# Sigmoid attention and two mixture layers on one core: PSUM banks, weight decoding and evictions rearranged

## The chip, the cores and the metric

The kernel runs on one core of a Trainium2 chip. The metric is the device time of one execution in microseconds (us). Engines are named as in the profile: PE is TensorE (matmuls; PEld its weight loads), DVE is VectorE, ACT is ScalarE, POOL is GpSimd, SP is SyncE, which here only issues transfers.

## The reference

Three stages follow each other. The inputs are fp32; batch 4, 12 heads, 448 positions, head size 64, so 1792 tokens of width 768.

```python
scores = q @ k.T / sqrt(64) - log(448);  x = sigmoid(scores) @ v      # per head
h = x @ w_in;  g = h - tanh(h);  x = g @ w_out                        # d_ff 2048, "layer one"
y = (sigmoid(x @ w_gate) * (x @ w_val)) @ w_out2                      # d_ff 1536, "layer two"
```

## The kernel before, in words

**Numbers.** Weights arrive as 64-bit floats and are read as pairs of 32-bit words. `decode()` (L114) turns a unit, a 128 x 768 part of a weight matrix, into fp32 words: piece a is one ScalarE pass (L121), b two VectorE passes (L124, L127), c two more (L133, L137) and the issue of a later unit's transfer. Matmuls run on fp32r pairs: each operand is kept as a high part (ScalarE copy) and a low part (operand minus high part), and each product is three matmuls (`mm3`, L300): high x high, high x low, low x high. `rounded()` (L145) makes the two parts of a weight, the low one by a GpSimd subtraction (L150).

**Attention** (24 head pairs) decodes the first seven units on the way. **Layer one** has 32 steps: 8 groups of two 128-column parts of `w_in`, for each of the four batches. Step i issues the hidden matmuls of step i+1 (`hidden_mm`, 36 matmuls, one PSUM tile of two banks), ScalarE's five passes for the activation (`hidden_act`, L322; squares, tanh, relu), and the output matmuls of step i: six groups of six matmuls (`project_group`, L370), each in one of four PSUM banks of the pool `psb`, each then added into an SBUF accumulator by VectorE (L381). Between the groups the list `extra` gives VectorE's pieces a to e of the activation and a decoding piece; f (L364), the low part of g, follows in the next step. Pieces run in program order on each engine.

**Layer two** has two passes over pairs of batches; each pass has six blocks. A block does seven products for the gate, then seven for the value (`TERMS`, nine matmuls each; the seven products replace eight, as in Strassen's scheme with Winograd's sums), and, spread over the gate half, twelve groups of six matmuls of the previous block's output projection ("fillers"). The operands s1 to s4 are sums and differences of halves of layer one's results (`operand`, L422); the weights t14, t32, b22 are differences made by VectorE (`ta`, `tb`). The four accumulators of a half lie in two tiles of two banks:

```python
pq = [psa.tile([128, 2, 512], F32, tag="pa", name=f"pq{j}") for j in range(2)]
pa, pb, pc, pe = (pq[j][:, i, :S] for j in range(2) for i in range(2))
bank = dict(a11=pa, s1=pe, s2=pb, a12=pa, s3=pc, s4=pb, a22=pc)
```

Sums shared by two products are copied from bank to bank by ScalarE (L575, L579 in `gate`; L593, L597 in `value`); VectorE closes a half with L583 and L585, or L599 to L611, and gg's low parts are two GpSimd subtractions of 128 x 896 (L606, L613).

In the first pass `background()` (L527), called after each product and each filler, hands out decoding pieces (`decode_pieces`) against a credit of time and at most one splitting piece (`split_pieces`) per call. A decoded pair of units is written to DRAM (`kept`, L471) and read again in the second pass (L476). Only pair 0 (two units) is decoded in the last steps of layer one. At the change of pass `turn()` makes the new operands, each in the place of one that is no longer needed.

Of the kernel before, what the change touches and what calls it, by code (L numbers as in the profile page):

```python
# [32 lines left out]
def kernel(  # L33
# [35 lines left out]
    stp = ctx.enter_context(tc.tile_pool(name="stp", bufs=2))  # L69
    dp = ctx.enter_context(tc.tile_pool(name="dp", bufs=1))  # L70
    psa = ctx.enter_context(tc.tile_pool(name="psa", bufs=2, space=bass.MemoryType.PSUM))
# [18 lines left out]
    MGAP = 16  # L90
    NPASS = NB // 2
# [13 lines left out]

    def fetch(u):
        if u >= len(units):
            return
        src, f = units[u]
        t = stp.tile([128, WC, 2], I32, tag="st", name=f"st{u}")  # L110
        nc.sync.dma_start(out=t.rearrange("p c w -> p (c w)"), in_=src[f])
        st_t[u] = t

    def decode(u, m):  # L114
# [28 lines left out]
        return [a, b, c]  # L143

    def rounded(w, mf, name, low=None):  # L145
# [4 lines left out]
        (low or nc.gpsimd).tensor_tensor(out=w1, in0=mf, in1=w0.bitcast(F32), op=ALU.subtract)  # L150

    def decode1(u):
# [7 lines left out]
        return decode(u, m) + [d]  # L160
# [161 lines left out]
    def hidden_act(i):  # L322
# [12 lines left out]
        nc.scalar.activation(out=uu, in_=h, func=AF.Square)  # L335
        nc.scalar.activation(out=y, in_=h, func=AF.Tanh)
        nc.scalar.activation(out=mk, in_=uu, func=AF.Relu, bias=gb[:, 2:3], scale=-1.0)
        nc.scalar.activation(out=s1, in_=mk, func=AF.Square, bias=gb[:, 0:1], scale=-1.0)
        nc.scalar.activation(out=s2, in_=mk, func=AF.Square, bias=gb[:, 1:2], scale=-1.0)
# [28 lines left out]
        return [a, b, c, d, e, f]  # L368

    def project_group(name, at, gt, outs, d, first, dst=None):  # L370

        po = psb.tile([128, 512], F32, tag="pb", name=name)
        for j, (_, w) in enumerate(outs):
            mm3(
                po[:, :S], lambda a: w[:, a, d], lambda a: gt[:, a, j],
                j == 0, j == len(outs) - 1,
            )
        if first:
# [8 lines left out]

    def groups1(i):

        g, t = divmod(i, NB)  # L390
        outs = [w_t[4 * g + 2], w_t[4 * g + 3]]
        gt = g_t.pop(i)
        if g == 0:
            acc[t] = acc_tile(t, f"acc{i}")
        for d in range(KD):
            def run(d=d):
                project_group(f"po{i}_{d}", acc[t], gt, outs, d, g == 0)
                if t == NB - 1 and d == KD - 1:
                    w_free.extend(n for n, _ in outs)
            yield run  # L400

    def project(i, extra):
        for group in groups1(i):
            group()
            if extra:
                extra.pop(0)()
        for f in extra:
            f()

# [11 lines left out]

    def operand(ps, term, low):  # L422
        a, b = acc[2 * ps], acc[2 * ps + 1]
        src = dict(
            a11=a[:, :KH], a12=a[:, KH:], a22=b[:, KH:], s1=b[:, :KH], s2=b[:, :KH],
# [3 lines left out]
        if term == "s1":  # L429
            nc.vector.tensor_tensor(out=b[:, :KH], in0=b[:, :KH], in1=b[:, KH:], op=ALU.add)  # L430
        elif term == "s2":
            nc.vector.tensor_tensor(out=b[:, :KH], in0=b[:, :KH], in1=a[:, :KH], op=ALU.subtract)
        elif term == "s3":
            nc.vector.tensor_tensor(out=a[:, :KH], in0=b[:, KH:], in1=b[:, :KH], op=ALU.subtract)
        elif term == "s4":
            nc.vector.tensor_tensor(out=b[:, :KH], in0=a[:, KH:], in1=b[:, :KH], op=ALU.subtract)
# [3 lines left out]
        low.tensor_tensor(out=t[:, 1], in0=src, in1=t[:, 0].bitcast(F32), op=ALU.subtract)  # L440

    m_t = {}
    kept = {}
    wk = {}
    done = {"slot": 0}
    decodes = []
    splits = []

    def pair_m(n):
        pool, tag = ((dp, "m"), (mp[0], "m2"))[n % 2]  # L450
        m_t[n] = pool.tile([128, 2 * WC], I32, tag=tag, name=f"mm{n}")
        return m_t[n]

    def decode_pieces(n):
        box = {}

        def start(h):
            if h == 0:
                pair_m(n)
            box[h] = decode(U2 + 2 * n + h, m_t[n][:, h * WC:(h + 1) * WC])  # L460

        def piece(h, s):
            def run():
                if s == 0:
                    start(h)
                box[h][s]()
                if h == 1 and s == 2:
                    done[n] = done["slot"]
                    if NPASS > 1:
                        kept[n] = keep_p.tile([128, 2 * WC], I32, tag=f"kept{n}", name=f"kept{n}")  # L470
                        nc.sync.dma_start(out=kept[n], in_=m_t[n])  # L471
            return run

        def again():
            pair_m(n)
            nc.sync.dma_start(out=m_t[n], in_=kept[n - 3 * NBLK])  # L476
            done[n] = done["slot"] + 3

        if n >= 3 * NBLK:
            return [(n, again, 0.0)]  # L480

        return [(n, piece(h, s), (0.2, 1.1, 1.9)[s]) for h in range(2) for s in range(3)]

    def split_pieces(n):
# [5 lines left out]
        def keep(key, lo, hi):  # L490
            def run():
# [9 lines left out]
                rounded(t, quarters(lo, hi), f"w{n}_{key}")  # L501
# [22 lines left out]
    credit = [0.0]  # L524
    last = [-9]

    def background(length):  # L527

        done["slot"] += 1
        now = done["slot"]  # L530
        credit[0] = min(credit[0] + length, 2.5)
        if splits:
            n, f, cost, room = splits[0]
            if n in done and done[n] + (cost > 0) < now and (not room or w_free):
                splits.pop(0)
                f()
                credit[0] -= cost
        while decodes and credit[0] > 0:
            n, f, cost = decodes[0]
            if any(s[0] <= n - 2 for s in splits):  # L540
                break
            decodes.pop(0)
            f()
            credit[0] -= cost
# [7 lines left out]
    def block(k, fillers):  # L552
# [4 lines left out]
        pa, pb, pc, pe = (pq[j][:, i, :S] for j in range(2) for i in range(2))  # L557
        bank = dict(a11=pa, s1=pe, s2=pb, a12=pa, s3=pc, s4=pb, a22=pc)

        def product(n, term):  # L560
            key, half = PRODUCT[term]
            s, w = wk[n, key]
# [10 lines left out]
        def gate(term):  # L573
# [6 lines left out]
            elif term == "a12":  # L580
                nc.scalar.activation(out=sg[0][:, 0], in_=pa, func=AF.Sigmoid)
            elif term == "s3":
                nc.vector.tensor_tensor(out=sg[1][:, 1], in0=pc, in1=p5[0], op=ALU.add)  # L583
            elif term == "s4":
                nc.vector.tensor_tensor(out=sg[0][:, 1], in0=pb, in1=p5[0], op=ALU.add)  # L585
                nc.scalar.activation(out=sg[1][:, 1], in_=sg[1][:, 1], func=AF.Sigmoid)
            elif term == "a22":
                nc.scalar.activation(out=sg[0][:, 1], in_=sg[0][:, 1], func=AF.Sigmoid)
                nc.scalar.activation(out=sg[1][:, 0], in_=pc, func=AF.Sigmoid)

        def value(term):
# [8 lines left out]
            elif term == "s3":  # L600
                nc.vector.tensor_tensor(out=pe, in0=pc, in1=p5[1], op=ALU.add)
            elif term == "s4":
                nc.vector.tensor_tensor(out=pb, in0=pb, in1=p5[1], op=ALU.add)
                nc.vector.tensor_tensor(out=sg[0][:, 1], in0=pb, in1=sg[0][:, 1], op=ALU.mult)
                nc.scalar.activation(out=gt[0][:, 0], in_=sg[0], func=AF.Copy)
                nc.gpsimd.tensor_tensor(  # L606
                    out=gt[0][:, 1], in0=sg[0], in1=gt[0][:, 0].bitcast(F32), op=ALU.subtract
# [251 lines left out]
```

## Time and profile before

| | us |
|---|---|
| median of 3 runs | 1260.87 (1260.05 to 1269.46) |
| the profiled execution's own time | 1250.63 |
| its span, first to last instruction | 1248.9 |
| PE busy | 1122.2 (90%) |
| DVE busy | 873.2 (70%) |
| ACT busy | 543.1 (43%) |
| POOL busy | 426.5 (34%) |

Times in rows are us from the span's start; durations of single instructions in groups are ns. A line such as `PE L302 MATMUL pq<-a,w_t ... [1.92 <-DVE sg L609]` says that TensorE stood idle for 1.92 us until VectorE's line 609 released it. PEclk is the granted share of TensorE's full clock (2.4 GHz; 0.5 is 1.2 GHz). A matmul's own duration overlaps with the next one's, so the pace is read from start to start.

### The profile page before, as it was taken

To read this page: it belongs to the slowest core of one execution; us is meant where nothing else is said; L and a number is where in the kernel's file an instruction comes from. 1 tells how busy PE (TensorE), PEld (TensorE's weight loads), DVE (VectorE), ACT (ScalarE), POOL (GpSimd) and SP (SyncE) were. 2 spreads that over 40 slices of the span, in tenths; PEclk is the share of its full clock that TensorE was granted. 3 is DMA by queue.
4 is the path that set the end of the run, shared out by engine and by line. 5 is a ranking of instruction groups with operands and counts; after the bars stand their busy time and mean duration, and the time that the engine had idled before them with its cause. 6 is when DMAs were issued, how large, how long until landed. Compare 5 with 4: busy or idle time off the path is not lost.

```text
span 1248.9 us, 15482 instructions
## 1 busy us (share of the span) xinstructions
PE 1122.2 (90%) x6085; PEld 995.5 (80%) x6085; DVE 873.2 (70%) x1150; ACT 543.1 (43%) x693; POOL 426.5 (34%) x288
## 2 busy tenths in 40 slices
PE   9999999999999999999566977877596899999998
PEld 5777799999999999988565866767485788988897
DVE  4778468888888888877886789678756444444343
ACT  6788535544445544444433333333325233323320
POOL 5555000111111111111663353435337555345431
PEclk9999999999999999999877989998998999999999
DMA  7666001111112111112034345442411322111202
GB/s 196 206 181 180 28 1 51 52 51 51 51 55 73 51 51 51 51 59 69 26 86 141 127 151 171 133 152 83 144 51 51 99 69 73 51 51 51 76 1 89
DMA packets 35017, 105.61 MB, mean 85 GB/s; under 512 B 5504, under 2 KB 20864, under 8 KB 34944
## 3 DMA queue, kind: packets, MB, share of 16 engines
q1 hardware_dynamic: 31712, 102.22, 25.4%
q0 software_dynamic: 3072, 2.17, 0.8%
q8 instruction: 48, 0.79, 0.2%
q14 instruction: 25, 0.20, 0.1%
q10 hardware_dynamic: 160, 0.23, 0.1%
HBM read 84.93 MB, written 19.66 MB: 84 GB/s over the span
## 4 chain that ended last, share of the span: by engine, by line
PE 69%; DVE 13%; issue 6%; ACT 4%; DMA 4%; POOL 4%; SPq 0%; ACTq 0%; POOLq 0%; DVEq 0%
PE pq L302 26%; PE po L302 17%; PE ph L302 17%; PE pv L286 4%; PE sa L251 3%; DVE mm L133 2%; POOL w_t L150 2%; DMA kept<-mm 2%; DVE mm L137 2%; DVE mm L124 1%; ACT mm L121 1%; PE sl L263 1%; DVE mm L512 1%; POOL w L150 1%; DMA st<-in_w_gate_dram 1%
## 5 line engine op out<-in xcount | busy, mean ns | idle before, releaser
L302 PE MATMUL po<-g,w 128*128 128x448 f32 x1152 | 238.4, 364 | 3.5 <-ACT g L361 2.3
L302 PE MATMUL ph<-x,w 128*128 128x448 f32 x1152 | 235.8, 362 | 0.2 <-ACT at L255 0.2
L302 PEld LDWEIGHTS po<-g,w 128*128 128x128 f32 x1152 | 217.4, 189 | 19.3 <-ACT g L361 2.7
L302 PEld LDWEIGHTS ph<-x,w 128*128 128x128 f32 x1152 | 215.8, 187 | 15.4 <-ACT at L255 0.6
L302 PE MATMUL pq<-gg,w 128*128 128x448 f32 x864 | 188.6, 368 | 4.3 <-DVE acco L381 2.6
L150 POOL TENSOR_TENSOR w<-m,w 128x768 fp32r<-128x768 f32 x32 | 59.3, 1853 | 381.1 <-ACT w L149 368.3
L302 PEld LDWEIGHTS pq<-gg,w 128*128 128x128 f32 x864 | 164.9, 191 | 18.0 <-DVE acco L381 4.2
L302 PE MATMUL pq<-s,w_t 128*128 128x448 f32 x648 | 147.9, 376 | 20.0 <-DVE y L360 8.9
L302 PEld LDWEIGHTS pq<-s,w_t 128*128 128x128 f32 x648 | 126.0, 196 | 32.8 <-ACT s L439 9.2
L381 DVE TENSOR_TENSOR acc<-po,acc 128x448 f32<-128x448 f32 x168 | 101.8, 618 | 52.8 <-PE po L302 52.8
L150 POOL TENSOR_TENSOR w_t<-mm,w_t 128x768 fp32r<-128x768 f32 x48 | 94.2, 1967 | 128.6 <-ACT w_t L149 128.6
L302 PE MATMUL pq<-a,w_b 128*128 128x448 f32 x432 | 106.8, 396 | 31.9 <-ACT pq L597 19.7
L302 PEld LDWEIGHTS pq<-a,w_b 128*128 128x128 f32 x432 | 89.1, 209 | 44.6 <-ACT pq L597 24.3
L381 DVE TENSOR_TENSOR acco<-pq,acco 128x448 f32<-128x448 f32 x120 | 72.7, 621 | 73.9 <-PE pq L302 73.9
L302 PE MATMUL pq<-a,w_t 128*128 128x448 f32 x216 | 59.4, 429 | 53.5 <-DVE sg L609 45.7
L302 PEld LDWEIGHTS pq<-a,w_t 128*128 128x128 f32 x216 | 46.7, 224 | 63.8 <-DVE sg L609 50.2
L150 POOL TENSOR_TENSOR w_b<-mm,w_b 128x768 fp32r<-128x768 f32 (+1 forms) x48 | 76.1, 1596 | 60.9 <-ACT w_b L149 58.6
L149 ACT ACTIVATE w_t<-mm 128x768 fp32r<-128x768 f32 x48 | 40.1, 841 | 103.2 <-DVE mm L512 61.8
L150 POOL TENSOR_TENSOR w<-mm,w 128x768 fp32r<-128x768 f32 x24 | 46.1, 1924 | 98.5 <-ACT w L149 78.8
L335 ACT ACTIVATE u<-ph 128x896 f32<-128x896 f32 x32 | 29.4, 918 | 115.9 <-PE ph L302 115.8
L255 ACT ACTIVATE at<-sa,bias_s 128x896 f32<-128x896 f32 x72 | 67.3, 1008 | 8.0 <-PE sa L251 8.0
L124 DVE TENSOR_SCALAR mm<-mm 128x768 f32<-128x768 f32 x36 | 32.9, 914 | 46.7 <-ACT mm L121 46.6
(90 smaller groups left out, 1634.0 us busy)
## 6 DMA issues: line engine op xcount, KB each, us to landing
st<-in_w_out_dram SPq DMA_DIRECT2D x28, 768.0 KB, 4.6
kept<-mm SPq DMA_DIRECT2D x18, 768.0 KB, 7.0
mm<-kept SPq DMA_DIRECT2D x18, 768.0 KB, 4.2
st<-in_w_in_dram SPq DMA_DIRECT2D x16, 768.0 KB, 4.4
st<-in_w_gate_dram SPq DMA_DIRECT2D x12, 768.0 KB, 4.4
st<-in_w_val_dram SPq DMA_DIRECT2D x12, 768.0 KB, 5.2
kt<-in_k_dram SPq DMA_DIRECT2D x48, 112.0 KB, 3.7
out_dram<-acco SPq DMA_DIRECT2D x24, 224.0 KB, 2.2
```

Of the source, the lines that this page charges most:

```text
L121: nc.scalar.activation(out=mf, in_=hi.bitcast(F32), func=AF.Abs)
L124: nc.vector.tensor_scalar(out=mf, in0=mf, scalar1=W_LOW, scalar2=W_HIGH, op0=ALU.max, op1=ALU.min)
L133: nc.vector.scalar_tensor_tensor(out=m, in0=hi, scalar=-0x40000000, in1=m, op0=ALU.bitwise_and, op1=ALU.bitwise_or,)
L137: nc.vector.scalar_tensor_tensor(out=m, in0=lo, scalar=29, in1=m, op0=ALU.logical_shift_right, op1=ALU.bitwise_or,)
L149: nc.scalar.activation(out=w0, in_=mf, func=AF.Copy)
L150: (low or nc.gpsimd).tensor_tensor(out=w1, in0=mf, in1=w0.bitcast(F32), op=ALU.subtract)
L251: nc.tensor.matmul(pa[:, j, :S], kk[r, ki, c], qq[r, qi], start=(i == 0), stop=(i == 2),)
L255: nc.scalar.activation(out=at[:, :, c], in_=pa[:, :, :S], func=AF.Sigmoid, bias=bias_s, scale=qk_scale,)
L286: nc.tensor.matmul(po[j * D:(j + 1) * D, h, :SH], vt[:, j, c], at[:, j, c, h * SH:(h + 1) * SH], start=False, stop=(c == NCH - 2),)
L302: nc.tensor.matmul(o, w(i), xv(j), start=first and n == 0, stop=last and n == 2, skip_group_check=seeded,)
L335: nc.scalar.activation(out=uu, in_=h, func=AF.Square)
L381: nc.vector.tensor_tensor(out=at[:, d], in0=po[:, :S], in1=at[:, d], op=ALU.add)
```

## The change

- **Banks.** `pa`, `pb`, `pc`, `pe` and the four banks of output groups become eight one-bank tiles of a new pool `pm`, opened after layer one. `gate` and `value` treat s3 and s4 in the order in which the products come; s3's two VectorE operations stand together.
- **Decoding.** All 36 units of layer two are listed in `early`, four pieces each (c is cut into c and c2). In layer one, steps 1 to 26 take a unit each, except those before step 24 whose number is a multiple of four; the rest is handed out by `background()`, one piece per call, then a pause of 4.0. Every decoded unit goes to DRAM and both passes read pairs by `load_m`. One staging buffer serves layer one's units and one layer two's (before: two for all).
- **Sums.** In layer one's steps 4 to 28, groups 1, 3 and 5 are seeded: ScalarE copies the accumulator into the PSUM bank ahead of the matmuls (`seed`) and copies the sum back (`post`), in place of VectorE's addition. ScalarE's passes of the activation are spread over the step.
- **GpSimd.** Subtractions of weights, gg and operands are cut in two or three; f moves from VectorE to GpSimd, b22's low part, some operands' and the last block's gg from GpSimd to VectorE.
- **Change of layer and pass.** s1 to s4 are sums of unchanged halves (`sums`) and are made earlier; fillers start after s2; `require()` makes a missing weight on the spot.

The core of the diff:

```diff
 def decode(u, m):
...
+        def c2():
             nc.vector.scalar_tensor_tensor(
                 out=m, in0=lo, scalar=29, in1=m,
...
-            fetch(u + 2)
+            fetch(follower(u))
...
 def rounded(w, mf, name, low=None):
...
-        (low or nc.gpsimd).tensor_tensor(out=w1, in0=mf, in1=w0.bitcast(F32), op=ALU.subtract)
+        for r in (slice(None),) if low else (slice(0, HC), slice(HC, None)):
...
 def hidden_act(i):
...
         def f():
-            nc.vector.tensor_tensor(
-                out=gt[:, 1], in0=y, in1=gt[:, 0].bitcast(F32), op=ALU.subtract
-            )
+            for j in range(2):
+                nc.gpsimd.tensor_tensor(
+                    out=gt[:, 1, j], in0=y[:, j], in1=gt[:, 0, j].bitcast(F32), op=ALU.subtract
+                )
...
+    def seed(name, at, d):
+        po = pb_tile(name)
+        nc.scalar.activation(out=po[:, :S], in_=at[:, d], func=AF.Copy)
+        return po
...
+    def step(i, act, dve, extra, po):
...
+        def pre(d):
+            if g and i < LASTSEED:
+                po[d] = seed(f"po{i}_{d}", at, d)
...
+        def post(d):
+            if i >= LASTSEED:
+                return
+            nc.scalar.activation(out=at[:, d], in_=po[d][:, :S], func=AF.Copy)
...
+        sq()
+        th()
+        group(0)
+        a()
+        pre(3)
+        cut()
+        group(1)
+        b()
+        run(ex[0] or [])
+        group(2)
+        q1()
+        post(1)
+        c()
+        run(ex[1] or [])
+        pre(5)
+        q2()
+        group(3)
+        d_()
+        run(ex[2] or [])
+        post(3)
+        group(4)
+        e()
+        run(ex[3] or [])
+        group(5)
+        post(5)
...
 def background(length, heavy=True):
...
+        if early and now > free_at[0]:
+            early.pop(0)()
+            if len(early) % 4 == 0:
+                free_at[0] = now + 4.0
...
 def block(k, fillers):
...
-        pa, pb, pc, pe = (pq[j][:, i, :S] for j in range(2) for i in range(2))
+        pa, pb, pc, pe = (
+            pm[0].tile([128, 512], F32, tag=f"p{c}", name=f"p{c}{k}")[:, :S] for c in "abce"
+        )
...
+        share = dict(s2=2, a12=4, s3=7, s4=10, a22=12)
...
+        def some(kind):
+            if early and len(early) % 4 == kind and (i < TAIL or kind) and (i % 4 or i > TAIL - 4):
+                early.pop(0)()
+
         for i in range(N1 - 1):
             hidden_mm(i + 1)
+            po = {}
+            if NB <= i < LASTSEED:
+                po[1] = seed(f"po{i}_1", acc[i % NB], 1)
             if todo:
                 todo.pop(0)()
             if rest:
                 rest.pop()()
             if todo:
                 todo.pop(0)()
-            extra = hidden_act(i + 1)
+            some(0)
+            some(3)
+            act, dve = hidden_act(i + 1)
...
+            if todo:
+                ex[0].append(todo.pop(0))
...
+                ex[2].append(todo.pop(0))
+            ex[1].append(lambda: some(2))
+            ex[2].append(lambda: some(1))
```

## Rows read from the trace of the kernel before

**Rows 1.** Windows: length, busy PE, PEld, DVE, ACT, POOL (counts), PEclk, DMA share, GB/s

```profile
146.00:560.00 414.00, 412.64 (x2080) 385.83 (x2081) 341.36 (x444) 199.67 (x222) 46.45 (x25) 1.00 0.14 48
560.00:601.00 41.00, 37.48 (x186) 34.20 (x185) 33.42 (x39) 22.26 (x24) 11.00 (x5) 1.00 0.19 58
601.00:680.00 79.00, 47.87 (x174) 41.07 (x173) 64.43 (x61) 26.29 (x36) 39.05 (x17) 0.76 0.31 100
680.00:855.00 175.00, 135.93 (x595) 119.01 (x595) 135.01 (x161) 60.78 (x90) 76.64 (x40) 0.90 0.42 135
...
1016.00:1229.00 213.00, 200.04 (x979) 183.92 (x978) 93.28 (x126) 66.64 (x103) 95.92 (x54) 0.99 0.13 45
```

**Rows 2.** TensorE's waits in layer two: us in total, times, longest

```profile
PE pq L302 <- DVE sg L609: 45.7, 12, 9.8
PE pq L302 <- ACT pq L597: 19.7, 12, 5.4
PE pq L302 <- ACT pq L579: 11.7, 2, 9.2
```

**Rows 3.** Timeline of the last block: start, us, engine, line [idle <-releaser]

```profile
1219.48 2.08 PE L302 MATMUL pq<-a,w_b 128*128 128x448 f32 x9 [0.68 <-ACT pq L597]
...
1227.08 2.57 PE L302 MATMUL pq<-a,w_t 128*128 128x448 f32 x9 [1.92 <-DVE sg L609]
...
1231.44 2.12 POOL L613 TENSOR_TENSOR gg<-sg,gg 128x896 fp32r<-128x896 f32 x1 [1.72 <-ACT gg L612]
```

**Rows 4.** Timeline of ScalarE: L575, once a block, of blocks 1, 5, 7, 11

```profile
679.96 0.53 ACT L575 ACTIVATE pq<-pq 128x448 f32<-128x448 f32 x1 [0.28 <-PE pq L302]
...
912.84 0.53 ACT L575 ACTIVATE pq<-pq 128x448 f32<-128x448 f32 x1
...
1015.66 0.53 ACT L575 ACTIVATE pq<-pq 128x448 f32<-128x448 f32 x1 [0.19 <-PE pq L302]
...
1188.24 0.53 ACT L575 ACTIVATE pq<-pq 128x448 f32<-128x448 f32 x1 [0.19 <-PE pq L302]
```

**Rows 5.** Decoding passes by line, layer two (mm) and before (m)

```profile
L133 DVE SCALAR_TENSOR_TENSOR mm<-st,mm 128x768 int32<-128x768 int32 x36 | 47.0, 1306 | 0.6
...
L127 DVE TENSOR_SCALAR mm<-mm 128x768 int32<-128x768 int32 x36 | 35.7, 992 | 1.2
...
L133 DVE SCALAR_TENSOR_TENSOR m<-st,m 128x768 int32<-128x768 int32 x32 | 30.4, 951 | 0.0
L121 ACT ACTIVATE m<-st 128x768 f32<-128x768 f32 x32 | 29.4, 917 | 52.6 <-POOL w L150 51.0 <-DMA st<-in_w_in_dram 1.6
...
L127 DVE TENSOR_SCALAR m<-m 128x768 int32<-128x768 int32 x32 | 17.9, 560 | 1.1
```

**Rows 6.** Timeline: a decoding pass beside GpSimd's subtractions

```profile
652.01 4.30 POOL L150 TENSOR_TENSOR w<-mm,w 128x768 fp32r<-128x768 f32 x2 [2.86 <-issue]
...
654.65 2.08 DVE L127 TENSOR_SCALAR mm<-mm 128x768 int32<-128x768 int32 x1
```

**Rows 7.** Timeline of one step of layer one

```profile
301.64 7.36 PE L302 MATMUL po<-g,w 128*128 128x448 f32 x36
...
305.48 1.03 ACT L339 ACTIVATE s<-mk,gb 128x896 f32<-128x896 f32 x1
...
312.47 1.09 DVE L364 TENSOR_TENSOR g<-y,g 128x896 fp32r<-128x896 f32 x1
...
316.04 7.36 PE L302 MATMUL po<-g,w 128*128 128x448 f32 x36
```

**Rows 8.** Timeline: first weight loads of two successive steps, end of layer one

```profile
563.29 0.19 PEld L302 LDWEIGHTS po<-g,w 128*128 128x128 f32 x1 [2.66 <-ACT g L361]
...
578.53 0.19 PEld L302 LDWEIGHTS po<-g,w 128*128 128x128 f32 x1
```

**Rows 9.** DMA issues: KB each, median us to landing

```profile
kept<-mm SPq DMA_DIRECT2D x18, 768.0 KB, 7.0
...
st<-in_w_gate_dram SPq DMA_DIRECT2D x12, 768.0 KB, 4.4
```

More of the change, by code (lines that the diff above doesn't have):

```diff
@@ L158, in d, with keeping, piece, run @@
             w_t[u] = n, w
-        return decode(u, m) + [d]
+        a, b, c, c2 = decode(u, m)
+        return [a, b, lambda: (c(), c2()), d]
+    kept = {}
+    early = []
+    def keeping(j):
+        box = []
+        def piece(s):
+            def run():
+                if s == 0:
+                    if late[0]:
+                        if not mq:
+                            mq.append(stp.tile([128, 2 * WC], I32, tag="st0", name="mq"))
+                        m = mq[0][:, j % 2 * WC:][:, :WC]
+                    else:
+                        m = wp.tile([128, WC], I32, tag="wh0", name=f"mk{j}")
+                    box.append(m)
+                    box.extend(decode(NU1 + j, m))
+                box[1 + s]()
+                if s == 3:
+                    n, h = divmod(j, 2)
+                    if h == 0:
+                        kept[n] = keep_p.tile([128, 2 * WC], I32, tag=f"kept{n}", name=f"kept{n}")
+                    nc.sync.dma_start(out=kept[n][:, h * WC:(h + 1) * WC], in_=box[0])
+                    whole.add(j)
+            return run
+        return [piece(s) for s in range(4)]
+    late = [False]
+    mq = []
+    whole = set()
     att_ctx = ExitStack()
@@ L424, in operand @@
         src = dict(
-            a11=a[:, :KH], a12=a[:, KH:], a22=b[:, KH:], s1=b[:, :KH], s2=b[:, :KH],
+            a11=a[:, :KH], a12=a[:, KH:], a22=b[:, KH:], s1=b[:, :KH], s2=a[:, :KH],
             s3=a[:, :KH], s4=b[:, :KH],
         )[term]
[L429 to L436, printed above, removed]
+        for other in (("s4", term) if term == "s3" else (term,)):
+            if other in ("s1", "s2", "s3", "s4") and (ps, other) not in summed:
+                sums(other, ps)
         t = x_tile(PLACE[ps][term], f"{term}_{ps}")
@@ L439, in operand, with load_m @@
         nc.scalar.activation(out=t[:, 0], in_=src, func=AF.Copy)
-        low.tensor_tensor(out=t[:, 1], in0=src, in1=t[:, 0].bitcast(F32), op=ALU.subtract)
+        for c in range(KH):
+            low.tensor_tensor(
+                out=t[:, 1, c], in0=src[:, c], in1=t[:, 0, c].bitcast(F32), op=ALU.subtract
+            )
     m_t = {}
-    kept = {}
     wk = {}
     done = {"slot": 0}
-    decodes = []
+    FETCH = 6.5
+    loads = []
     splits = []
-    def pair_m(n):
-        pool, tag = ((dp, "m"), (mp[0], "m2"))[n % 2]
-        m_t[n] = pool.tile([128, 2 * WC], I32, tag=tag, name=f"mm{n}")
[L452 to L482, printed above, removed]
+    order = [0, 1]
+    for blk in range(NK):
+        order += [n for n in (3 * blk + 3, 3 * blk + 2, 3 * blk + 4) if n < 3 * NK]
+    place = {n: at for at, n in enumerate(order)}
+    def load_m(n):
+        pool, tag = ((dp, "m"), (mp[0], "m2"))[place[n] % 2]
+        m_t[n] = pool.tile([128, 2 * WC], I32, tag=tag, name=f"mm{n}")
+        k = n % (3 * NBLK)
+        assert 2 * k + 1 in whole
+        nc.sync.dma_start(out=m_t[n], in_=kept[k])
+        done[n] = done["slot"] + FETCH
     def split_pieces(n):
@@ L633, in block @@
                 turn(ps + 1, term)
-            background(1.8 - {"a12": 0.6, "s3": 0.6, "s4": 1.8, "a22": 0.6}.get(term, 0.0))
+            background(1.8, term not in ("s4", "a22"))
             value(term)
@@ L721 @@
         assert not todo
[L722 removed]
+        for f in dve[3:]:
             f()
```

277 lines of the change are left out of this document (182 added, 95 removed).

## The prediction

> **What bounds the kernel now.** I read the stages first, then TensorE's waits, then the waits' places. A step of layer one does 72 matmuls; in steady state it takes 14.40 us, 0.200 us a matmul, and TensorE is busy without a gap and at the full clock (2.4 GHz, granted 1.00) [rows 1, 7]. Nothing is to be gained there. Layer two is another matter: 12 blocks of 198 matmuls plus the 36 left from layer one are 2,412 x 0.200 = 482 us, and it takes 1248.9 - 601 = 648 us. So 166 us lie in it, at VectorE's expense: its share of the time is 82% (64.43 of 79) and 77% (135.01 of 175) in the first pass, 44% (93.28 of 213) in the second [rows 1]. The start times of one copy per block (L575) give the profile of the loss: the first pass takes (912.84 - 679.96) / 4 = 58.2 us a block, the two blocks around the change of pass (1015.66 - 912.84) / 2 = 51.4, the second pass (1188.24 - 1015.66) / 4 = 43.1 [rows 4]. 198 x 0.200 = 39.6 would be the pace of TensorE alone. The entry is worst: 601 to 680 for 162 matmuls (32.4 us) and one product more (1.8).
>
> TensorE's waits name two lines above all: 45.7 us for L609 and 19.7 + 11.7 for the copies L597 and L579 [rows 2]. What these two wait for is not what the products need: the product a22 adds into pc, L609 reads pe; a12 adds into pa, the copies read pb and write pc. But pa, pb share one tile and pc, pe the other. In the last block, with VectorE idle enough, it costs 0.68 and 1.92 us still [rows 3].
>
> **The change, part by part.** *Banks.* With a tile for each accumulator, a22 waits only for L601, two VectorE operations and one product earlier; a12 only for the copy of pa, done one product (1.8 us) before. In the second pass 0.68 + 1.92 go from each value half, and up to 0.3 comes back: 43.1 becomes 40.2 a block, 39.6 plus 0.6 for the odd late copy. Order s3/s4 within gate() and value() now follows the order of the products, which puts no new wait in. What is late next is the true wait, a22 on L601, hidden as long as VectorE isn't over 1.2 us (1.8 - 0.62) late.
>
> *Decode.* A weight half (unit) costs VectorE four passes: 2 x 0.56 + 2 x 0.95 = 3.0 us in layer one, 2 x 0.99 + 2 x 1.31 = 4.6 in layer two [rows 5]. They are the same operations; the longer ones ran beside a GpSimd subtraction (L127: 2.08 us instead of 0.56, while L150 runs on GpSimd) [rows 6]. So far all but two of 36 units' passes fall in layer two, 6 a block, 27.6 us of VectorE in 58.2. The change decodes one unit in each step from 1 to 26 whose number isn't a multiple of four, and from 24 on in each: 21. 15 are left, one per about 10 us of background() time (four calls, then 4.0): some 3.9 a block, over in block 4, ahead of use (pair 10 is first needed by block 3). VectorE's sum in a first-pass block: 135.01 / 175 x 58.2 = 44.9 now; less 27.6, plus 3.9 units at 3.8 (midway, since GpSimd's pieces are half as long) = 14.8, plus 1 for the subtractions of b22 that move to it: 33, of 43.6 that I take for these blocks (75%, the same share as now at 58.2, where false waits added to it; 40.2 and 50 are the ends). Blocks 1 to 3: 43.6; block 4: 41.6.
>
> *Entry.* Here s1 and s2 are summed late; one wait for L579, the copy that follows the product s2, takes 9.2 us [rows 2]. The sums now come ahead of the last step, the four halves of weights are split two steps earlier, no unit is decoded in the first 16 us. I take 5 us of loss (0 to 15): 32.4 + 1.8 + 5 = 39 for the 79. *Change of pass.* The low parts of the operands for s1 to a22 (1,344 columns each) are cut in three, and s1's, s2's and s4's go to VectorE, which has decoding no more. 102.8 for two blocks becomes 87 (80.4 to 97).
>
> Layer two: 39 + 3 x 43.6 + 41.6 + 87 + 4 x 40.2 + 57.3 (the last 60.7 less 2.9 for its value half and 0.5 for VectorE's faster last low part) = 516.5 of 648: **-131**.
>
> *Layer one pays.* Per step, in effective pace: VectorE loses three of six evictions (0.54 each from start to start) and the low part of g (1.0), and gets a unit (3.0) in three of four steps. Now it is busy 341.36 / 414 = 82%, 11.9 us a step on the mean [rows 1], 12.4 in the steps that decode a unit for layer one (25 of the 29); then 12.4 - 1.6 - 1.0 + 3.0 = 12.8, below 14.4. ScalarE: 199.67 / 414 x 14.4 = 6.9 now, plus three seeds and three copies (0.53 each, the size of L575 [rows 4]) and 0.9 for the unit's first pass [rows 5]: 11.0. It too fits. What counts is the order. In the step of [rows 7], counted from the first group's start (301.64), the last square ends at 4.87, g's low part is done at 11.92 and needed at 14.40: 2.5 us to spare. In the changed queue the seeds of groups 3 and 5, group 1's copy back and a weight half's copy stand ahead of the last square (some 0.45 each and 0.75 from start to start): it ends at 7.0. Behind it come, on VectorE, one operation of 1.0, a unit's pass of 0.95, an eviction of 0.55 and the predicated copy of 1.1: 10.6; ScalarE's copy, 1.0: 11.6; two GpSimd pieces of 1.05 (a 128x896 subtraction takes 2.12 [rows 3]): 13.7. The second piece is needed at 15.0, after the group's first three matmuls. 1.3 us are to spare; what exceeds them TensorE waits, in every step anew.
>
> Two things can eat them. First, GpSimd's pieces and VectorE's decoding collide right there. [rows 6] show VectorE held until the subtraction ends. The Trainium skill, "SBUF — State Buffer", section "Who interferes with whom", says that a VectorE operation with two SBUF inputs and a GpSimd operation that reads SBUF exclude each other for the whole instruction, whoever starts first. By that rule moving g's low part speaks against this change: up to 2.1 us a step more for VectorE, 12.8 + 2.1 = 14.9, or 0.5 x 21 = 11 us in all. Second, the next unit's first pass stands on ScalarE ahead of the squares, and needs a transfer issued when the unit before is done (single buffers): 4.4 us, and the write-back of the decoded half, 7.0 for twice its size [rows 9]. The unit is done at about 9; with 4.4 and 0.9 the squares can start at 14.3, in time; with 7.0 and 0.9 at 16.9, 2.5 us late, in the 15 steps that follow a step with a unit. Queued behind it on ScalarE are the squares, the seeds and the copies; TensorE waits for these at the next group. Ends: 0, and 15 x 2.5 + 11 = about 48 with nothing to spare. I take **+8**: 1.3 us are to spare, and a step of four is free to catch up. A gain is excluded: TensorE has no gap there now. Edits without a price: attention (same two staging buffers until unit 6), the pools' new names.
>
> Own time of the profiled execution: 1250.6 - 131 + 8 = 1127.6. The median of the three runs shown is 1260.9, 10 above; forecast: **1138 us**.
>
> **Rivals.** *Layer one becomes the slower stage*: the transfer loop above decides in every step with a unit, +40 in place of +8: 1170. For it: a tail step that decodes for layer two already stretched to 578.53 - 563.29 = 15.24, the weight load waiting 2.66 for ScalarE's g [rows 8]. Against: there the pieces stood between every two operations. Chance 0.17. *VectorE stays the bound in the first pass*: 15 units and GpSimd's locks keep blocks 1 to 3 at 50, entry 45, block 4 at 46, the pass change at 97: +40, 1178. For it: 75% busy is much for an engine that is waited for in order. Chance 0.11. *The banks don't do what they say*: the wait passes on to L601 and to the copies, whose own lateness is the true cause; second-pass blocks stay at 43.1, first-pass ones lose 3 more each: 6 x 2.9 + 4 x 3 = 29, 1167. Against: in [rows 3] VectorE and ScalarE were free. Chance 0.10. *Slower than before*: layer one falls from the full clock. Now it runs at 1.00; where TensorE waits, 601 to 680, the granted clock is 0.76, a mean of stretches at 2.4 and at 1.2 GHz [rows 1]. A step at 0.76 takes 14.4 / 0.76 = 18.9; with 1 us of waiting +5.5 over 27 steps: +149 instead of +8, 1279. It decides from 131 / 27 = 4.9 us a step on. Against: the tail, with the wait of [rows 8], kept 1.00 (560 to 601) [rows 1]. Chance 0.04.
>
> **How the numbers follow.** The forecast holds 0.58: 1138, alone between 1115 and 1160 (first-pass blocks at 40.2 or 46, entry 0 to 15, layer one 0 to 15). The range takes in the three rivals' 1167 to 1178 and some of their sum: 1108 to 1190. About 1% of the time (12 us) is what a measurement of this kernel can tell from no change. All cases but the last are over 5% faster; the last, and a mixture of the first two rivals at their ends, give the rest: faster 0.94, same 0.02, slower 0.04.
>
> **What would show it.** Right: no wait on the line that succeeds L609, no a12 wait on the copy into pc; second-pass blocks at 40 to 40.5; first-pass ones at 42 to 46 with VectorE near 75%; TensorE's gap at the entry below 10 us; layer-one steps of 14.4 to 15 with VectorE about 88% and ScalarE 77% busy, GpSimd's waits beside c2. Wrong: layer-one steps above 15.5, or a granted clock below 1.00 there; first-pass blocks at 50; a22 waiting over 1 us for VectorE in the second pass.

## The result, and the profile after

The changed kernel takes 1127.72 us (median of 4 runs, 1127.19 to 1131.71), the kernel before 1260.46 (four runs; the 1260.87 above is of three): a ratio of 0.894, 95% interval 0.889 to 0.899. The forecast was 1138. The profiled execution has a span of 1125.4 us at a mean granted clock of 0.998 (before: 1248.9 at 0.959).

By stage, with the windows of the changed kernel (columns as in [rows 1]): layer one's middle, blocks 1 to 4, and the second pass.

```profile
142.00:530.00 388.00, 378.16 (x1872) 339.49 (x1871) 318.40 (x369) 252.95 (x358) 133.19 (x94) 1.00 0.31 100
661.00:824.00 163.00, 158.50 (x783) 146.20 (x784) 127.92 (x166) 69.39 (x104) 102.17 (x82) 1.00 0.46 154
910.00:1068.00 158.00, 158.00 (x792) 148.09 (x791) 77.18 (x112) 57.76 (x89) 85.12 (x80) 1.00 0.17 61
```

The counts of matmuls tell the pace: 388 / 1872 = 0.207 us in layer one, which was 0.199 before (414 / 2080 of [rows 1]); 158 / 792 = 0.199 in the second pass, where TensorE has no gap left. In the first pass some matmuls are missing from the trace (783 for four blocks of 198), so its pace is read from the marks below: 40.7 for a block's 198, 0.206 each.

The same marks as in [rows 4], from the timeline: the first product of layer two on TensorE, then L722 (L575 before) of blocks 1, 5, 7 and 11; the last line is the first product of layer two in the kernel before.

```profile
619.50 1.96 PE L365 MATMUL pa<-a,w_b 128*128 128x448 f32 x9
...
661.48 0.52 ACT L722 ACTIVATE pb<-pa 128x448 f32<-128x448 f32 x1
...
824.43 0.52 ACT L722 ACTIVATE pb<-pa 128x448 f32<-128x448 f32 x1
...
909.91 0.52 ACT L722 ACTIVATE pb<-pa 128x448 f32<-128x448 f32 x1
...
1068.31 0.52 ACT L722 ACTIVATE pb<-pa 128x448 f32<-128x448 f32 x1
```

```profile
601.18 1.97 PE L302 MATMUL pq<-a,w_b 128*128 128x448 f32 x9
```

| stretch, us | before | forecast | after |
|---|---|---|---|
| start to first product of layer two | 601.2 | 609 | 619.5 |
| entry and block 0, to block 1's L722 | 79 | 39 | 42.0 |
| blocks 1 to 4, mean of one | 58.2 | 43.1 | 40.7 |
| blocks 5 and 6 together | 102.8 | 87 | 85.5 |
| second pass, a block | 43.1 | 40.2 | 39.6 |
| last block's L722 to the end | 60.7 | 57.3 | 57.1 |

Layer two takes 506 us (forecast 516.5, before 648); layer one 18.3 more than before (forecast 8).

TensorE's waits from 618 on (us in total, times, longest). [rows 2] had 45.7, 19.7 and 11.7 at its head:

```profile
PE pc L365 <- DVE pe L761: 5.1, 3, 2.2
PE pb L365 <- ACT pb L722: 2.7, 4, 1.2
PE pq L365 <- POOL gg L742: 2.4, 2, 1.8
```

In layer one (145 to 600), ScalarE's wait for a transfer and the longest of the weight loads:

```profile
ACT mk L145 <- DMA kept<-mk: 40.8, 15, 3.9
...
PEld po L365 <- DVE acc L472: 10.9, 13, 1.1
PEld po L365 <- POOL g L437: 8.5, 20, 0.7
PEld po L365 <- ACT po L454: 3.8, 15, 1.1
```

Fifteen times ScalarE waited for the write-back of a decoded half: there are 15 steps with a unit that follow a step with a unit. One such step in the timeline: the write-back is issued at 318.05; ScalarE's pass for the next unit (L145, L121 before) starts at 323.69, and only then the first square (L399).

```profile
308.98 0.91 ACT L399 ACTIVATE u<-ph 128x896 f32<-128x896 f32 x1
...
318.05 0.43 SPq L215 DMA_DIRECT2D kept<-mk  x1
...
320.38 3.75 POOL L437 TENSOR_TENSOR g<-y,g 128x448 fp32r<-128x448 f32 x2 [5.49 <-issue]
...
321.32 1.79 DVE L163 SCALAR_TENSOR_TENSOR m<-st,m 128x768 int32<-128x768 int32 x1
...
323.69 0.89 ACT L145 ACTIVATE mk<-st 128x768 f32<-128x768 f32 x1 [2.57 <-DMA kept<-mk]
324.49 0.90 ACT L399 ACTIVATE u<-ph 128x896 f32<-128x896 f32 x1
...
338.89 0.92 ACT L399 ACTIVATE u<-ph 128x896 f32<-128x896 f32 x1 [2.27 <-PE ph L365]
```

The step from 308.98 to 324.49 takes 15.51, the next one, without a unit ahead of it, 14.40. The two GpSimd pieces of g take 3.75 together and VectorE's last decoding pass beside them 1.79 instead of 0.95.

A late unit's four passes on VectorE, by line (L148, L151, L157, L163 were L124, L127, L133, L137), 630 to 830:

```profile
L157 DVE SCALAR_TENSOR_TENSOR mq<-st,mq 128x768 int32<-128x768 int32 x15 | 21.1, 1410 | 0.1
...
L163 DVE SCALAR_TENSOR_TENSOR mq<-st,mq 128x768 int32<-128x768 int32 x15 | 17.4, 1163 | 0.1
L151 DVE TENSOR_SCALAR mq<-mq 128x768 int32<-128x768 int32 x15 | 16.2, 1079 | 0.5
L148 DVE TENSOR_SCALAR mq<-mq 128x768 f32<-128x768 f32 x15 | 12.2, 817 | 4.0 <-ACT mq L145 4.0
```

Together 4.47 us, beside 4.6 in [rows 5] and the 3.8 of the forecast. What the length of the pieces does to it is tested below.

### The profile page after: what moved, and what is told of

It reads as the page before. It is cut to its first block, busy times and chain, and to the rows that moved or that the text cites. A ratio compares the mean times of both kernels' runs of the same rounds, so it can differ in the third digit from the quotient of the medians.

```text
span 1125.4 us, 15990 instructions
## 1 busy us (share of the span) xinstructions
PE 1091.5 (97%) x6085; PEld 967.6 (86%) x6085; DVE 806.8 (72%) x1083; ACT 608.8 (54%) x855; POOL 522.7 (46%) x475
## 4 chain that ended last, share of the span: by engine, by line
PE 60%; DVE 14%; ACT 9%; DMA 9%; issue 5%; POOL 3%; SPq 1%; ACTq 0%; DVEq 0%; POOLq 0%
PE pq L365 14%; PE ph L365 10%; DMA kept<-mk 8%; PE pb L365 6%; PE po L365 6%; PE pa L365 6%; PE pc L365 5%; PE pv L349 5%; PE sa L314 4%; PE pe L365 3%; DVE ph L422 2%; DVE ph L427 2%; ACT mk L405 1%; ACT y L402 1%; PE sl L326 1%
## 5 line engine op out<-in xcount | busy, mean ns | idle before, releaser
L365 PE MATMUL po<-g,w 128*128 128x448 f32 x1152 | 247.7, 367 | 10.3 <-DVE acc L472 6.0
L365 PEld LDWEIGHTS po<-g,w 128*128 128x128 f32 x1152 | 211.7, 188 | 40.5 <-POOL g L437 11.6
L365 PEld LDWEIGHTS ph<-x,w 128*128 128x128 f32 x1152 | 215.8, 187 | 15.3 <-ACT at L318 0.6
L437 POOL TENSOR_TENSOR g<-y,g 128x448 fp32r<-128x448 f32 x64 | 114.0, 1801 | 194.8 <-issue 166.1
L178 POOL TENSOR_TENSOR w_t<-mm,w_t 128x384 fp32r<-128x384 f32 x92 | 101.1, 1128 | 119.7 <-ACT w_t L175 54.1
L178 POOL TENSOR_TENSOR w<-m,w 128x384 fp32r<-128x384 f32 x64 | 63.6, 1017 | 113.2 <-ACT w L175 80.9
L365 PE MATMUL pa<-a,w_b 128*128 128x448 f32 x432 | 94.2, 362 | 0.0
L365 PEld LDWEIGHTS pa<-a,w_b 128*128 128x128 f32 x432 | 81.0, 187 | 5.4
L472 DVE TENSOR_TENSOR acc<-po,acc 128x448 f32<-128x448 f32 x93 | 57.3, 618 | 26.6 <-PE po L365 26.6
L178 POOL TENSOR_TENSOR w<-mm,w 128x384 fp32r<-128x384 f32 x44 | 48.5, 1124 | 45.5 <-ACT w L175 43.3
L742 POOL TENSOR_TENSOR gg<-sg,gg 128x448 fp32r<-128x448 f32 x44 | 62.5, 1451 | 12.3 <-ACT gg L739 12.3
L178 POOL TENSOR_TENSOR w_b<-mm,w_b 128x384 fp32r<-128x384 f32 x46 | 51.3, 1138 | 23.1 <-ACT w_b L175 12.1
L349 PE MATMUL pv<-at,vt 128*64 128x224 f32 x576 | 61.0, 362 | 0.0
```

Of the source, the lines that this page charges most:

```text
L178: (low or nc.gpsimd).tensor_tensor(out=w1[:, r], in0=mf[:, r], in1=w0[:, r].bitcast(F32), op=ALU.subtract)
L349: nc.tensor.matmul(po[j * D:(j + 1) * D, h, :SH], vt[:, j, c], at[:, j, c, h * SH:(h + 1) * SH], start=False, stop=(c == NCH - 2),)
L365: nc.tensor.matmul(o, w(i), xv(j), start=first and n == 0, stop=last and n == 2, skip_group_check=seeded,)
L437: nc.gpsimd.tensor_tensor(out=gt[:, 1, j], in0=y[:, j], in1=gt[:, 0, j].bitcast(F32), op=ALU.subtract)
L472: nc.vector.tensor_tensor(out=at[:, d], in0=po[:, :S], in1=at[:, d], op=ALU.add)
L742: low.tensor_tensor(out=gt[t][:, 1, j], in0=sg[t][:, j], in1=gt[t][:, 0, j].bitcast(F32), op=ALU.subtract,)
```

## The experiments

"The changed kernel" is the 1127.7 above; runs of before taken beside these runs have medians from 1255.1 to 1258.7, so a difference of 4 us between two runs is about as small as can be told. "The first product" is that of layer two on TensorE, at 619.5 in the changed kernel: it dates the end of layer one.

**Pairs again.** The changed kernel with two accumulators to a tile:

```diff
-        pa, pb, pc, pe = (
-            pm[0].tile([128, 512], F32, tag=f"p{c}", name=f"p{c}{k}")[:, :S] for c in "abce"
-        )
+        pq = [pm[0].tile([128, 2, 512], F32, tag=f"q{c}", name=f"q{c}{k}") for c in "ac"]
+        pa, pb, pc, pe = (pq[j][:, i, :S] for j in range(2) for i in range(2))
...
```

> The changed kernel with its accumulators in pairs again: pa, pb in one two-bank tile, pc, pe in another, all else as changed (the eight banks' places are kept as far as pairs allow). Theory (waits across a tile of two banks held TensorE): the second-pass block goes from 39.6 back to 42.2 (0.68 + 1.92 per value half), the first-pass blocks by 3 to 8 us each, since VectorE is 90% busy there and late; in all +35 to +65 us, and the waits of a22 on the second multiplication of s4 and of a12 on the copy into pc come back. Rival (these waits only pass on to the true ones): within +10 us.

1139.3 us, 11.6 more: a miss, far below the range and just above the rival's 10. TensorE's waits from 618 on, and the copy L721 (L722) of blocks 10 and 11:

```profile
PE qa L365 <- ACT qc L752: 8.1, 12, 0.7
PE qc L365 <- DVE sg L761: 4.7, 3, 2.9
```

```profile
1039.34 0.53 ACT L721 ACTIVATE qa<-qa 128x448 f32<-128x448 f32 x1
...
1079.90 0.52 ACT L721 ACTIVATE qa<-qa 128x448 f32<-128x448 f32 x1
```

```profile
1067.81 1.97 PE L365 MATMUL qa<-s,w_t 128*128 128x448 f32 x9
1070.46 2.07 PE L365 MATMUL qa<-a,w_b 128*128 128x448 f32 x9 [0.68 <-ACT qc L752]
1072.37 1.96 PE L365 MATMUL qc<-s,w_t 128*128 128x448 f32 x9
```

The wait of a12 on the copy into pc is back in each of 12 blocks, at the 0.68 of [rows 3]; the second-pass block takes 40.56, 0.96 more than in the changed kernel. The wait costs more than its own length: from the product ahead of it to the one behind it 4.56 us pass, where two products at 1.80 take 3.60. The wait of a22 is not back there (L761 in this run is the multiplication that was L609). The changed order does that: it now stands right behind the addition, before s4's operations, and is over when a22 comes.

**Banks alone.** The kernel before, with one-bank tiles in the same places and nothing else (the edit is the one above, reversed).

> The kernel before with one edit: each of the four accumulators (and each of the four group banks) gets a one-bank tile of its own, at the same place in PSUM; the decoding stays in layer two. Theory (false waits cost what TensorE's waits name, but the first pass stays held by VectorE's 45 us a block of decoding): second-pass blocks at 39.7 to 40.3 in place of 43.1, first-pass blocks 3 to 6 us shorter than 58.2, in all 35 to 55 us faster than before. Rival (the waits carry the whole first-pass loss, VectorE's share none): first-pass blocks below 46, 75 to 100 us faster.

1226.7 us, ratio to before 0.977 (0.974 to 0.981), about 28 us, below the range. TensorE's waits from 601 on (L611 and L593 are the lines that were L601 and L583), and L585 (the L575 of this kernel) of blocks 1, 4, 7 and 11:

```profile
PE pc L303 <- DVE pe L611: 35.1, 6, 10.8
PE pc L303 <- DVE sg L593: 13.5, 5, 6.7
```

```profile
678.65 0.53 ACT L585 ACTIVATE pb<-pa 128x448 f32<-128x448 f32 x1
...
853.36 0.53 ACT L585 ACTIVATE pb<-pa 128x448 f32<-128x448 f32 x1
...
1005.60 0.53 ACT L585 ACTIVATE pb<-pa 128x448 f32<-128x448 f32 x1
...
1164.16 0.53 ACT L585 ACTIVATE pb<-pa 128x448 f32<-128x448 f32 x1
```

Second pass: (1164.16 - 1005.60) / 4 = 39.6, at the lower end of what was expected. First pass: (853.36 - 678.65) / 3 = 58.2, not a microsecond less, where 3 to 6 were expected. There the wait passed on from L609 to L601 (L611 here), the addition that a22 does need: in blocks 1 to 3, a22 waited three times in both kernels, 15.4 us in all for the one and 18.0 for the other. VectorE was late, and a22 waited for it under either name.

**No passes.** What made VectorE late? As the last run, without the four decoding passes of layer two's units:

```diff
         def b():
+            if u >= 4 * G1:
+                return
...
         def c():
+            if u >= 4 * G1:
+                fetch(u + 2)
+                return
```

> The kernel before with one-bank accumulators, and without VectorE's four decoding passes for layer two's 36 units (the ScalarE pass, the transfers in, out and back, the splits and all products stay; the weights of layer two are not decoded). The banks alone left the first-pass blocks at 57.9 us. Theory (VectorE's decoding is the first pass's loss): first-pass blocks fall to 40 to 43, the entry and block 0 by 15 to 30 us, in all 95 to 125 us less than with the banks alone. Rival (the chain from fetch over ScalarE to GpSimd and back holds the blocks): first-pass blocks stay above 48.

1142.5 us, 84 less than with the banks alone (the range began at 95). L590 (L575) of blocks 1 and 5, and the window between them:

```profile
653.76 0.52 ACT L590 ACTIVATE pb<-pa 128x448 f32<-128x448 f32 x1
...
825.68 0.52 ACT L590 ACTIVATE pb<-pa 128x448 f32<-128x448 f32 x1
```

```profile
653.80:825.70 171.90, 163.74 (x800) 150.80 (x801) 79.10 (x105) 79.59 (x121) 91.95 (x52) 0.98 0.53 175
```

(825.68 - 653.76) / 4 = 43.0 us a block, with VectorE 46% busy and a granted clock of 0.98. So the passes are most of the first pass's loss: 15.2 of the 18.6 us by which a block exceeded 39.6. The transfers and ScalarE's passes, which stayed, are not. Part of the 15.2 may be the clock, which was 0.90 in the first pass before [rows 1]: 39.6 / 0.90 less 39.6 / 0.98 makes 3.6 us, an estimate. Entry and block 0 (first product to L575 of block 1) take 55.6, where they took 75.7 with the banks alone. The change of pass gains nothing (96.4 for blocks 5 and 6, beside 95.5).

**The write-back's hold.** In layer one the write-back sends other data of the same size, so the buffer is free at once:

```diff
-                    nc.sync.dma_start(out=kept[n][:, h * WC:(h + 1) * WC], in_=box[0])
+                    held = box[0] if late[0] else x[0][0].bitcast(I32)[:, 0, :2, :384]
+                    nc.sync.dma_start(
+                        out=kept[n][:, h * WC:(h + 1) * WC] if late[0]
+                        else kept[n][:, h * WC:(h + 1) * WC].rearrange("p (a c) -> p a c", a=2),
+                        in_=held,
+                    )
```

> In layer one the write-back of a decoded half sends as many bytes from a finished attention operand instead of the decoded buffer, so the buffer is free for the next unit at once; the 21 decoded halves are not stored. Theory (transfer loop: the next unit's first ScalarE pass waits for the write-back, with squares, seeds and copies queued behind it): the 40.8 us of ScalarE waits on that transfer fall below 15 (the fetch still lands late), layer-one steps of 15.5 become 14.4 to 14.9, the time falls by 8 to 18 us. Rival (GpSimd and VectorE excluding each other in the same place set the step): within 4 us of the changed kernel.

1112.4 us, 15.3 less than the changed kernel. Layer one's middle in the windows, and ScalarE's longest remaining wait for a transfer:

```profile
142.00:530.00 388.00, 384.94 (x1940) 352.29 (x1939) 335.87 (x384) 264.25 (x373) 139.05 (x98) 1.00 0.34 105
```

```profile
ACT mk L145 <- DMA st<-in_w_out_dram: 9.5, 6, 1.8
```

388 / 1940 = 0.200 us a matmul: layer one is back at TensorE's pace. The first product starts at 603.89. The remaining waits, for fetches, sum to 24.3 over three rows, more than the expected 15, but none is over 2.1 us, and the pace shows that they hardly delay TensorE.

**Two buffers.** The same effect without leaving anything out; the second buffer is the idle half of the one that layer one's decoding uses:

```diff
-        m = dp.tile([128, WC], I32, tag="m", name=f"m{u}", padded_shape=[128, 2 * WC])
+        if not m1:
+            m1.append(dp.tile([128, 2 * WC], I32, tag="m", name="m1"))
+        m = m1[0][:, :WC]
...
-                        m = wp.tile([128, WC], I32, tag="wh0", name=f"mk{j}")
+                        if j % 2:
+                            m = m1[0][:, WC:]
+                        else:
+                            m = wp.tile([128, WC], I32, tag="wh0", name=f"mk{j}")
```

> The changed kernel with two buffers for the decoded halves in layer one (every second one in the idle half of the buffer that layer one's decoding uses), so that the next unit doesn't wait for the write-back. It computes all that the changed kernel computes. Transfer loop theory: as in the run that leaves the write-back's hold out, 8 to 18 us faster than the changed kernel, steps of 14.4 to 14.9. Rival: within 4 us.

1113.3 us, 14.4 less than the changed kernel. In the timeline of a step like the one above, the next unit's pass now waits for its fetch alone:

```profile
312.60 0.43 SPq L221 DMA_DIRECT2D kept<-m  x1
...
317.28 0.91 ACT L145 ACTIVATE mk<-st 128x768 f32<-128x768 f32 x1 [1.63 <-DMA st<-in_w_val_dram]
...
318.10 0.90 ACT L405 ACTIVATE u<-ph 128x896 f32<-128x896 f32 x1
```

It starts 4.68 us after the issue of the write-back, not 5.64. The first product starts at 603.66: of the 18.3 us that layer one had lost, 15.8 are back.

**g's low part on VectorE**, in one piece, as before the change:

```diff
-            for j in range(2):
-                nc.gpsimd.tensor_tensor(
-                    out=gt[:, 1, j], in0=y[:, j], in1=gt[:, 0, j].bitcast(F32), op=ALU.subtract)
+            nc.vector.tensor_tensor(out=gt[:, 1], in0=y, in1=gt[:, 0].bitcast(F32), op=ALU.subtract)
```

> The low part of g in layer one on VectorE again, in one piece, in place of two GpSimd pieces; all else as changed. VectorE gets 1.09 us a step, and loses the collision of the last decoding pass with the GpSimd pieces (0.84). Theory (the transfer loop sets the step, the lock is second): time within 6 us of the changed kernel, TensorE's waits on GpSimd's g gone. Rival (the lock sets it): 8 to 20 us faster. Third (VectorE's sum sets it, 12.8 + 1.0 with waits above 14.4): 8 to 25 us slower.

1123.9 us, 3.8 less: the first theory. The first product starts 2.4 earlier, at 617.12. VectorE's last decoding pass, 1.79 beside the GpSimd pieces, is back at 0.96; the weight loads no longer wait for GpSimd, but more for VectorE:

```profile
L163 DVE SCALAR_TENSOR_TENSOR m<-st,m 128x768 int32<-128x768 int32 x25 | 24.0, 958 | 0.9
```

```profile
PEld po L365 <- DVE acc L471: 14.2, 13, 1.1
```

With both edits (two buffers, and this one):

> Two buffers for decoded halves (as in the run before) and the low part of g on VectorE in one piece. It computes all that the changed kernel computes. Expected from the two runs apart: 1113.3 less the 4 us that the second edit gave = 1108 to 1111, if its gain lies around the ends of layer one and in layer two; if VectorE's sum (12.8 + 1.0 us a step) now sets layer one's step, 1113 to 1120.

1110.6 us, ratio to before 0.885 (0.880 to 0.889), 17.1 below the changed kernel: the first of the two cases. The first product starts at 601.73. The two edits give back all but half a microsecond of what layer one had lost.

**No seeds.** All of layer one's sums by VectorE (`pre` and `post` do nothing, group 1 isn't seeded):

```diff
-            by_act = d % 2 == 1 and i < LASTSEED
+            by_act = False
```

> All of layer one's sums by VectorE again: no seeds and no copies back on ScalarE, six additions a step on VectorE; all else as changed. By the prediction's sums VectorE then has 12.8 + 1.6 = 14.4 us a step besides the collision of 0.8: steps of 15.5 to 16.5, 10 to 30 us slower than the changed kernel. Rival (ScalarE's queue, 2.1 us longer by the seeds, sets the step): 5 to 15 us faster.

1135.5 us, 7.8 more, just below the range. The window 142 to 530:

```profile
142.00:530.00 388.00, 370.86 (x1834) 335.34 (x1834) 358.93 (x431) 189.06 (x214) 120.99 (x92) 0.99 0.31 98
```

388 / 1834 = 0.212 a matmul, VectorE 93% busy. The route over ScalarE is worth about 0.3 us a step.

**Fewer units early.** A unit in every second step (13), 23 left, which are handed out faster in layer two (a pause of 1.0 in place of 4.0, beginning at 2.0 in place of 16.0):

```diff
-            if early and len(early) % 4 == kind and (i < TAIL or kind) and (i % 4 or i > TAIL - 4):
+            if early and len(early) % 4 == kind and (i < TAIL or kind) and i % 2:
...
-                free_at[0] = now + 4.0
+                free_at[0] = now + 1.0
...
-        free_at[0] = 16.0
+        free_at[0] = 2.0
```

> A unit in every second step of layer one (13 units in place of 21; none follows another step's), 23 left for layer two with a pause of 1.0 in place of 4.0. Transfer loop theory: layer one's steps fall to 14.4 to 14.8, 8 to 15 us less there. Layer two: 8 units more at 4.5 us for a VectorE that is 90% busy, over five blocks: 7 us a block if VectorE sets the pace (35 us), 0 to 2 if TensorE does. Expected together: 5 to 25 us slower than the changed kernel; a gain of 5 to 15 would say that the pace of the first pass is TensorE's.

1145.4 us, 17.7 more. Layer one gained a little more than expected (the first product starts at 602.60, 16.9 earlier; 388 / 1944 = 0.200 in the same window); layer two lost twice that: L722 of blocks 1 and 4, and the window between.

```profile
653.25 0.52 ACT L722 ACTIVATE pb<-pa 128x448 f32<-128x448 f32 x1
...
800.68 0.52 ACT L722 ACTIVATE pb<-pa 128x448 f32<-128x448 f32 x1
```

```profile
653.00:801.00 148.00, 126.11 (x589) 112.80 (x590) 126.09 (x160) 59.13 (x89) 82.08 (x63) 0.97 0.61 195
```

(800.68 - 653.25) / 3 = 49.1 a block, VectorE 85% busy. The same three blocks of the changed kernel (block 4 has no decoding left there) take (785.61 - 661.48) / 3 = 41.4, with VectorE 88% busy:

```profile
661.50:785.60 124.10, 120.69 (x594) 110.75 (x594) 109.00 (x138) 54.85 (x83) 81.04 (x63) 1.00 0.55 182
```

So the busy share doesn't tell the two apart. VectorE's sum does: 126.09 / 3 = 42.0 us a block, which is more than TensorE's 39.6, against 109.00 / 3 = 36.3.

The other direction, a unit in every step from 1 to 26 (26 units, 10 left), on top of two buffers and g's low part on VectorE:

```diff
-            if early and len(early) % 4 == kind and (i < TAIL or kind) and (i % 4 or i > TAIL - 4):
+            if early and len(early) % 4 == kind and (i < TAIL or kind) and i:
```

> As the run with two buffers and g's low part on VectorE, with a unit of layer two in each of layer one's steps 1 to 26 (26 units, 10 left). Layer two gains at most 1.2 us in each of four blocks (40.8 to 39.6). Layer one loses its free steps: if VectorE's 13.8 us and its waits exceed 14.4 in a row of steps, 0.3 to 0.8 us a step, 8 to 20 us slower than that run; if not, 2 to 5 us faster.

1109.4 us, 1.2 below the run with both edits, which these runs can't tell from nothing: neither of the two cases. In the traces a gain and a loss nearly cancel: blocks 1 to 4 take 40.0 us each in place of 40.8, and the first product starts 2.3 later, at 604.02.

**Long pieces.** GpSimd's subtractions uncut.

```diff
-        for r in (slice(None),) if low else (slice(0, HC), slice(HC, None)):
+        for r in (slice(None),):
```

and likewise for f, gg and the operands.

> GpSimd's subtractions in one piece again (weights 768 columns, gg and g 896, operands 1,344), on the same engines as in the changed kernel. The prediction priced a late unit at 3.8 us because pieces are half as long. Theory after the result (late units took 4.5 as before, so the length matters little for VectorE, and somewhat for what waits behind GpSimd): 3 to 15 us slower, most of it in layer one, where g's low part comes 1 us later. Rival (short pieces carry the first pass): 20 us or more slower, first-pass blocks above 45.

1140.6 us, 12.9 more, in the range but not in the expected place. TensorE's longest waits from 618 on:

```profile
PE pc L365 <- DVE pe L757: 13.2, 4, 4.7
PE pb L365 <- ACT pb L720: 6.2, 3, 3.9
```

It is layer two that loses, the first pass above all (L757 is the addition L761 of the changed kernel): the first product starts at 619.66, as with short pieces, and blocks 1 to 3 take (797.60 - 665.08) / 3 = 44.2, 2.8 more each. Their window:

```profile
665.00:797.60 132.60, 123.47 (x604) 113.52 (x602) 116.18 (x138) 55.21 (x82) 63.48 (x31) 0.99 0.50 169
```

A late unit's four passes take 5.01 us here in place of 4.47, and VectorE's sum rises to 116.18 / 3 = 38.7 us a block, from 36.3. At the same time VectorE can be held longer just ahead of an addition that TensorE needs (up to 4.7 us there). Which of the two costs the 2.8 us, no run here tells apart.

**Another place for pe.**

```diff
-        for c in "abc01e23":
+        for c in "abce0123":
```

> The changed kernel with the eight banks in another order: pe lies in the fourth bank, where the last hidden tile of layer one stands until the activation is done with it, and output banks follow; nothing else differs. Theory (before, the product s1 waited 8.9 us for L360, the last reader of that tile, and not for its operand): the entry, from the last first square to the first copy, stays near 10, TensorE then waits 5 to 10 us ahead of s1, the time grows by 5 to 10 us. Rival (the wait was for the operand's sum): within 2 us.

1127.4 us, 0.3 less: nothing. The wait is there under its old name, and costs 0.9:

```profile
PE pe L365 <- DVE y L432: 0.9, 1, 0.9
```

The theory falls in its size: before, TensorE waited 8.9 us for that reader (L360) because the reader was late, at 610.7, nearly 10 us behind the first product; in the changed kernel it is on time.

## Why the prediction was right, and where not

The net of the steps was right almost to the microsecond (-123 forecast for the profiled execution, 1127.6; 1127.3 measured), but by two errors that cancel: layer two gained 10.6 us more than forecast, layer one lost 10.3 more. That closeness is luck. The ten between 1138 and 1127.7 came from carrying over the distance of before's median from its profiled execution; the changed kernel has none.

*Banks.* Right for the second pass (40.2 forecast, 39.6). Wrong in the part that the false waits had in the first pass: "where false waits added to it". They added nothing there; with one-bank tiles alone the wait went to L601. That is the rival "the wait passes on", true for one pass and false for the other. I also gave the reordering of s3 and s4 no gain; the run with pairs shows that it alone removes a22's wait in the second pass. And the second-pass block gained 3.5 us where the two waits sum to 2.6: the run with pairs shows that such a wait costs more than its length.

*Decode.* VectorE's sum in blocks 1 to 3 was forecast at 33 us a block and measures 36.3, in part because a late unit cost 4.47 us and not the 3.8 taken for it. Even so these blocks took 41.4 and not 43.6. The step that failed is from the sum to the block's time: I scaled by the busy share (75% of 43.6), and the share was 88%. The runs follow the sum instead: 36.3 us of work fit under TensorE's 39.6 with little loss (41.4), 38.7 take 44.2 (long pieces), 42.0, more than 39.6, take 49.1 (fewer units early), and 45 took 58, in the old order and at a clock of 0.90. Without any passes the old order still took 43.0, so the sum is not all; what makes up for that in the changed kernel (pieces, order, earlier sums) was tested for the pieces alone.

*Entry* 42.0 (39) and *change of pass* 85.5 (87) came out within 3 us. Of the entry's 37 us the decoding passes can explain 20 (75.7 with the banks alone, 55.6 without the passes); the cause of the rest is settled only in so far as it is not the bank of pe.

*Layer one.* The mechanism was named: ScalarE's first pass waiting for the write-back, with the squares behind it, in 15 steps. Its size was wrong: 8 of a bound of 48. Two runs that take the hold away win 15.3 and 14.4 us, so the loop is most of the 18.3; with g's low part on VectorE as well, all but half a microsecond is back. The step that failed is "1.3 us are to spare, and a step of four is free to catch up". The GpSimd pieces took 3.75 and not 2.1, and VectorE's L163 took 1.79 beside them; without them it takes 0.96. These figures agree with the rule of the Trainium skill ("SBUF — State Buffer", section "Who interferes with whom") that a VectorE operation with two SBUF inputs and a GpSimd operation that reads SBUF exclude each other. The 1.65 us more are over the 1.3 to spare. But putting g's low part back on VectorE won only 2.4 us in layer one while the loop stood (388 / 1877 = 0.207 a matmul), and 1.9 without the loop: the delay also reaches TensorE through VectorE's additions, which free the group's banks, and through the seeds. I counted what is to spare at one of three places. Nor can a free step give back what TensorE has already lost, where its pace is the bound. The shares forecast for layer one, VectorE 88% and ScalarE 77%, came out at 82 and 65 (318.40 and 252.95 of 388).

## What to carry to other kernels

A wait that a profile names is worth what the next wait in the same place leaves of it: where the engine that releases is late itself, removing a false dependency renames the wait, and its gain shows only where that engine has time. Work moved under a saturated engine is paid for at the tightest loop that it closes (here pass, decoding, write-back, buffer, next pass: longer than a step), so go round that loop once with a transfer's landing in it before asking for busy shares; a second buffer was worth 14 us here. The busy share of an in-order engine says little of what it costs, because it is a share of a time that the engine's own lateness has stretched (88% in blocks of 41.4 us, 85% in blocks of 49.1): compare the sum of its work in a stretch with the time that the bounding engine needs for it (36.3 and 42.0 us against 39.6 here).

## What the runs showed of the hardware

A write-back of 384 KB landed in 5.6 us in the median, beside a 768 KB fetch issued 0.4 us before it (4.3 to 5.0), where one of 768 KB had taken 7.0 [rows 9]: half the size is not half the time.

```profile
kept<-mk SPq DMA_DIRECT2D x21, 384.0 KB, 5.6
```

TensorE's clock, at 0.76 and 0.90 in the windows of [rows 1], is granted in full (1.00) in all the windows of the changed kernel shown above; where the waits went, the clock came back with them, also in the run without decoding passes (0.98 in blocks 1 to 4).
